# Small operations moved from VectorE to GpSimd and ScalarE in the middle of a decode block's forward and backward pass, and one buffer handed over an iteration later

## The chip, the cores and the metric

The kernel runs on one core of a Trainium2 chip. A core has five engines with an instruction queue each, worked off in order: TensorE (PE in the profile, with its weight loads as PEld), VectorE (DVE), ScalarE (ACT), GpSimd (POOL) and SyncE (SP). The engines wait for each other by semaphores. Transfers between the chip's memory (HBM) and the core's on-chip memory go through 16 DMA engines; they are issued from the queues of SP (loads), POOL (the two big gradients) and ACT (the smaller gradients). PE writes to PSUM, here eight banks; the other data lie in SBUF.

The metric is the device time of one execution in microseconds, as the median of several runs.

## The reference

The program computes a transformer block for two sequences at one new token each, and the gradients of its output. With B = 2, H = 32 heads, S = 4096 cached positions and a head size of 128:

```python
q = (layernorm(x) @ wq)                      # per head, 128 long
scores = einsum("bhqd,bhkd->bhqk", q, k) * Dh**-0.5
p = softmax(scores)
o = einsum("bhqk,bhkd->bhqd", p, v)
h = x + o @ wo
h2 = h + relu(layernorm(h) @ w1) @ w2
# outputs: h2, and the gradients for x, k_cache, v_cache, wq, wo, w1, w2
```

The caches are 2 x 32 x 4096 x 128 in bfloat16, 64 MB each. Both are read, and gradients of the same size are written: for a head, the gradient of V is the outer product of the probabilities `p` with the output's gradient `go`, and the gradient of K that of `p * (V go - p.(V go))` with q.

## The kernel before, in words

A head's K or V is one tile of 128 partitions x 32 blocks x 128 (1 MB). There are 64 pairs of batch and head.

**First pass.** `p1_iter(i, ...)` is a generator that interleaves three pairs: pair `i` (its K tile is transposed by PE in four groups, `pair_transpose`, copied from PSUM by ScalarE, and multiplied with q, `pair_matvec`, to give the scores `s` and the row maximum `rmax`), pair `i-1` (PE spreads the maximum, `mx`; VectorE reduces it to `nb`; ScalarE makes `ep` = exp; VectorE makes `pk` = K times e in two halves of 16 blocks, `pk_half(0)` and `pk_half(1)`; the copy of e into `pk`'s extra column, `pk_tile`, is done by GpSimd before iteration `P2_AT` and by ScalarE from there on; `P_bf` keeps e for later), and pair `i-2` (PE multiplies V with `pk`, eight calls of `m_part`, into the single bank `m`, and sums `u` in `u_part`; ScalarE copies the result out as `MT` and `OU`). The generator yields eight times an iteration, at positions k = 0 to 7. The K tile of pair `i-1` is given back after `pk_half(1)`, the V tile of pair `i-2` at the end.

**The middle.** After the 32 pairs of batch 0 a background generator, `middle_gen(0)`, computes the rest of the forward pass for this batch and the beginning of the backward pass: the output projection, the second layernorm, the MLP, and then groups of heads, `go_group`, which turn the gradient of the attention's output into `goc`, `gom` (through `pair_rows`: two small PE products and four copies out of PSUM), `negdot` and `GQc`. Its large VectorE instructions are the multiply-and-sum rows of `ttr`; how many of them go into an iteration is set by `slot`. `o_group` scales four heads' outputs.

**Second pass.** It begins at iteration `P2_AT` = 41, with one turn `j` in two iterations: `p2_iter` makes `rb` and `pp`, the products of V with `go`, and gV in two halves of VectorE; `p2_tail` makes `gsp` and gK in two halves. GpSimd issues the write of a gradient tile as soon as VectorE has made its second half. When the first pass has ended (iteration 65), the second goes on alone, with the weights' gradients beside it. The V tiles of the last six heads of batch 0 are kept from the first pass, so that the first turns load nothing.

**What sets the order.** The program is written out by hand in the order in which each engine shall work: `plan` pairs iterations `i` with turns `j`, and the tables `LIGHT`, `HEAVY` and `HEAVY_TAIL` say after which position k of an iteration a step of the second pass is put. Thirteen 1 MB buffers are shared by the tags "ld" (loads) and "g" (gradients); `give(tile, to)` hands a buffer to a tag, and `pump()` issues loads in a fixed order as far as "ld" has buffers, in the order in which they were given back. A load waits on SyncE until its buffer's last reader is done.

`p1_iter` and `pk_half` are at lines 483 and 495 of the kernel before, `pair_rows` at 348, `o_group` at 621, `go_group` at 701, and the main loop's choice of positions at 1278.

Of the kernel before, what the change touches and what calls it, by code (L numbers as in the profile page):

```python
# [7 lines left out]
FP32 = mybir.dt.float32  # L8
BF16 = mybir.dt.bfloat16
ALU = mybir.AluOpType  # L10
ACT = mybir.ActivationFunctionType
# [4 lines left out]
def kernel(  # L16
# [20 lines left out]
    nc = tc.nc  # L37

    B, Sq, D = A_x.shape
    _, H, Sk, Dh = A_k_cache.shape  # L40
# [4 lines left out]
    NSC = Sk // 128  # L45
# [3 lines left out]
    SCALE = 0.08837890625  # L49
# [3 lines left out]
    HALF = NSC // 2  # L53
    GH = 8
    OG = 4
# [12 lines left out]
    small = ctx.enter_context(tc.tile_pool(name="small", bufs=3))  # L68
# [5 lines left out]
    def pst(shape, dtype, role, name):  # L74

        k = banks[role].pop(0)
        banks[role].append(k)
        return ps.tile(shape, dtype, tag=f"bank{k}", bufs=1, name=name)
# [19 lines left out]
    def goes_to(tag):  # L98

        if owned[tag] > wanted.get(tag, len(pools)):  # L100
            for other in homes:
                if owned[other] < wanted.get(other, 0):
                    return other
        return tag

    def give(t, to=None, first=False):
        tag, k, _ = home_of.pop(id(t))
        to = to or goes_to(tag)
        owned[tag] -= 1
        owned[to] += 1  # L110
        free[to] += 1
        homes[to].insert(0 if first else len(homes[to]), k)
        given_at[k] = step[0]
# [86 lines left out]
    OFc = cols.tile([128, H, B], BF16)  # L200
    GQc = cols.tile([128, H, B], BF16)
    qsc = cols.tile([128, H, B], BF16)
    goc = cols.tile([128, H, B], BF16)

    gom = cols.tile([128, B, H, 2, 2], BF16)
    nc.gpsimd.memset(gom[:], 0.0)
    qm = gom
    negdot = cols.tile([128, H, B], FP32)
    OU = cols.tile([128, B, H], FP32)
    Uc = cols.tile([128, B, H], FP32)  # L210
    rt = cols.tile([128, B, H], FP32)
    asum = cols.tile([128, B, ND], FP32)
    nc.vector.memset(asum[:], 0.0)
    P_bf = cols.tile([128, NPS, NSC], BF16)
# [130 lines left out]
    w1_t = wts.tile([128, ND, Dff], BF16)  # L345
    wo_r = A_wo.rearrange("(c p) d -> p c d", p=128)

    def pair_rows(dst, src, hs, bs):

        n, nb = hs.stop - hs.start, bs.stop - bs.start  # L350
        t = pst([128, 2, n, nb], FP32, "mid", "pr_ps")
        for par in range(2):
            nc.tensor.matmul(t[:, par, :, :], lhsT=sel[:, par, :, :].rearrange("p c k -> p (c k)"),
                             rhs=src[:, hs, bs], start=True, stop=True)
        for c in range(2):
            rows = slice(64 * c, 64 * c + 64)
            for par in range(2):
                nc.vector.tensor_copy(out=dst[rows, bs, hs, par, c].rearrange("p b h -> p h b"), in_=t[rows, par, :, :])

    WO_PARTS = (0, H // 4, H // 2, 3 * H // 4, H - OG, H)  # L360

# [47 lines left out]
    NP1 = len(pairs)  # L409
# [6 lines left out]
    p_slot = {bh: n for n, bh in enumerate(pairs[:NPS])}  # L416
# [66 lines left out]
    def p1_iter(i, dve_group, busy):  # L483

        c = S1[i] if i < NP1 else None
        p = S1[i - 1] if 1 <= i <= NP1 else None
# [7 lines left out]

        def pk_half(k):

            sl = slice(k * HALF, (k + 1) * HALF)
            nc.vector.tensor_tensor(  # L498
                out=p["pk"][k][:, :, 0:128].rearrange("p s (a two) -> p s a two", two=2),
                in0=p["K"][:, sl, :].rearrange("p s (a two) -> p s a two", two=2),  # L500
                in1=p["ep"][:, sl, None, :].to_broadcast([128, HALF, 64, 2]), op=ALU.mult)

        def pk_tile(k):

            pk = pkp.tile([128, HALF, 130], BF16, tag="pK", bufs=3, name="pk")
            col, e = pk[:, :, 128:129], p["ep"][:, k * HALF:(k + 1) * HALF, 0:1]
            if i < P2_AT:
                nc.gpsimd.tensor_copy(out=col, in_=e)  # L508
            else:
                nc.scalar.copy(out=col, in_=e)  # L510
            p["pk"].append(pk)
# [12 lines left out]
        if c is not None:  # L524
            b, h = pairs[i]
# [4 lines left out]
        if r is not None:  # L530
            r["m"] = pst([128, 132], FP32, "m", "m_ps")
        m_first = r is not None and H + 1 < i < P2_AT + 3
        if m_first:
            m_part(0)
        if p is not None:

            bp, hp = pairs[i - 1]
# [9 lines left out]
        if p is not None:  # L547
            ep = pkp.tile([128, NSC, 2], BF16, tag="ep", bufs=3, name="ep")
            nc.scalar.activation(out=ep[:], in_=p["s"][:, :, None].to_broadcast([128, NSC, 2]),  # L549
                                 func=ACT.Exp, bias=nb[:], scale=SCALE, accum_out=es[:, bp, hp:hp + 1])  # L550
# [9 lines left out]
        if p is not None:  # L560
            pk_half(0)
# [18 lines left out]
        if p is not None:  # L580
            pk_tile(1)
            if hp % OG == OG - 1:
                nc.vector.reciprocal(out=rt[:, bp, hp + 1 - OG:hp + 1], in_=totp)
            (nc.gpsimd if i < P2_AT else nc.vector).tensor_copy(out=P_bf[:, p_slot[(bp, hp)], :], in_=ep[:, :, 0])
            pk_half(1)
            give(p["K"], "g" if i in (P2_AT, NP1) else None, i == NP1)
        if r is not None:
            m_part(5)
            m_part(6)
# [31 lines left out]
    def o_group():  # L621
        b, g = divmod(o_next[0], H // OG)
        hs = slice(g * OG, g * OG + OG)
        nc.vector.tensor_tensor(out=OU[:, b, hs], in0=OU[:, b, hs], in1=rt[:, b, hs], op=ALU.mult)
        nc.vector.tensor_copy(out=OFc[:, hs, b], in_=OU[:, b, hs])
        o_next[0] += 1

    def a_group():
# [10 lines left out]
    def a_heads(i):  # L639
# [3 lines left out]
        if o_next[0] < NP1 // OG and i >= o_next[0] * OG + OG + 2:  # L643
            b, g = divmod(o_next[0], H // OG)
            if i >= (O_AT[g] if b == 0 else P2_AT + 2):
                o_group()
# [37 lines left out]
    def ttr(in0, in1, acc, width, kc=128, junk=None):  # L684
        if junk is None:
            junk = rows3[:, 0, :]
        nc.vector.tensor_tensor_reduce(out=junk[0:kc, 0:width], in0=in0, in1=in1, scale=1.0, scalar=0.0,  # L687
                                       op0=ALU.mult, op1=ALU.add, accum_out=acc)
# [3 lines left out]
    def turn():  # L692

        while slot[0] <= 0:
            yield 0.0
        slot[0] -= 1
# [4 lines left out]
    def go_group(b, h0, h1, hbc):  # L701

        hs = slice(h0, h1)
        n = h1 - h0
        go32 = small.tile([128, GH], FP32, tag="go32", bufs=1, name="go32")
        for k in range(n):
            yield from turn()
            ttr(wo_t[:, h0 + k, :], hbc, go32[:, k:k + 1], D)
            yield 0.9
        nc.vector.tensor_copy(out=goc[:, hs, b], in_=go32[:, 0:n])  # L710
        pr = small.tile([128, GH], FP32, tag="pr", bufs=1, name="pr")
        nc.vector.tensor_tensor(out=pr[:, 0:n], in0=goc[:, hs, b], in1=OU[:, b, hs], op=ALU.mult)
        yield from wait(2 + b)
        pair_rows(gom, goc, hs, slice(b, b + 1))
        yield from wait(2)
        d_ps = pst([128, 2, GH], FP32, "mid", "d_ps")
        nc.tensor.matmul(d_ps[:, 0, 0:n], lhsT=ones_f32, rhs=pr[:, 0:n], start=True, stop=True)
        for k in range(n):
            h = h0 + k
            MT, side, slot_mt = MTs.pop((b, h))  # L720
            nc.tensor.matmul(d_ps[:, 1, k:k + 1], lhsT=MT[:], rhs=goc[:, h, b:b + 1], start=True, stop=True)
            mt_free[side].append(slot_mt)
        nc.vector.tensor_scalar(out=negdot[:, hs, b], in0=d_ps[:, 0, 0:n], scalar1=-1.0, scalar2=None, op0=ALU.mult)
        ud = small.tile([128, GH], FP32, tag="ud", bufs=1, name="ud")
        nc.vector.tensor_tensor(out=ud[:, 0:n], in0=Uc[:, b, hs], in1=negdot[:, hs, b], op=ALU.mult)
        mg = small.tile([128, GH], FP32, tag="mg", bufs=1, name="mg")
        nc.vector.tensor_tensor(out=mg[:, 0:n], in0=d_ps[:, 1, 0:n], in1=rt[:, b, hs], op=ALU.mult)
        nc.vector.tensor_tensor(out=ud[:, 0:n], in0=mg[:, 0:n], in1=ud[:, 0:n], op=ALU.add)
        nc.vector.tensor_scalar(out=GQc[:, hs, b], in0=ud[:, 0:n], scalar1=SCALE, scalar2=None, op0=ALU.mult)
        for h in range(h0, h1):  # L730
            done.add(("go", b, h))
        yield
# [154 lines left out]
    NSB = 8  # L887
# [251 lines left out]
    def bg_until(mark):  # L1139
        slot[0] = 99  # L1140
        forced[0] = True
        while mark not in done:
# [2 lines left out]

    M0_ITERS = 7
    P2_AT = H + 2 + M0_ITERS
    E0 = H - KEPT[0] + 3
    EARLY_T = {E0: [(0, 0)], E0 + 1: [(0, 1), (1, 0)], E0 + 2: [(0, 2)], E0 + 3: [(0, 3)],
               E0 + 4: [(1, 1)], E0 + 5: [(1, 2)], E0 + 6: [(1, 3)]}  # L1150
    RATES = (0.2, 0.8, 0.2, 0.8, 0.45)
# [4 lines left out]
    i = j = 0  # L1156
    while i <= NP1 + 1 or j <= NP1:
        ii = i if i <= NP1 + 1 else None
        jj = j if i >= NP1 or (i >= P2_AT and (i - P2_AT) % 2 == 0) else None
        plan.append((ii, jj))  # L1160
# [45 lines left out]
    HEAVY = {1: 1, 3: 1, 4: 1, 5: 1, 7: 1}  # L1206
    HEAVY_TAIL = {1: 1, 2: 1, 3: 1, 4: 1, 5: 1, 7: 1}
    LIGHT = {1: 1, 3: 1, 6: 1}
# [8 lines left out]
    for n, (i, j) in enumerate(plan):  # L1217
# [21 lines left out]
        open_tail = [k for k in S2 if "T3" in S2[k]]  # L1239
# [25 lines left out]
        if i is None:  # L1265
            spread[0] = 2
            at_k[0] = 1
            k = 0
# [6 lines left out]
                bg_step(1, RATE2[(0, 2, 0, 1)[sum(j >= a for a in RATE2_AT)]] * (0.4 if spreading[0] else 1.0))  # L1275
                bg_step(2, RATE3)
            continue
        at = LIGHT if j is None else HEAVY_TAIL if open_tail else HEAVY
        for k, _ in enumerate(p1_iter(i, i < H + 1, 0)):
            for _ in range(at.get(k, 0)):  # L1280
                if g2 is not None:
# [60 lines left out]
```

## Time and profile before

| | us |
|---|---|
| median of 3 runs | 893.32 |
| lowest and highest of them | 891.46, 894.52 |
| the profiled execution | 890.47 |
| its span, first to last instruction | 888.7 |

| engine | busy us | share of the span |
|---|---|---|
| PE | 731.7 | 82% |
| DVE | 687.7 | 77% |
| ACT | 469.3 | 53% |
| POOL | 203.9 | 23% |

The DMA engines moved 361.84 MB, 407 GB/s in the mean over the span; HBM was read for 211.11 MB and written for 149.13 MB. The granted clock of TensorE was 0.781 of full speed in the mean, 1.0 or nearly so up to some 440 us and 0.5 to 0.7 later.

Iteration i can be found in the trace by its instruction `nb`: iteration 37's starts at 233.58 us, that of 41 at 258.62, that of 45 at 287.60. An iteration of the first pass in the middle takes 5.9 to 6.7 us.

A line of a timeline gives the start and the duration in us, the engine, the kernel's line, the operation, output and inputs by their names in the program, the shapes, and in brackets how long the engine had been idle before and what ended this. An instruction's end can overlap the start of the next on the same engine. The profile of one execution is the source of all durations.

### The profile page before, as it was taken

How to read it: one execution, taken by the hardware profiler on the slowest of the kernel's cores; microseconds unless marked ns; L12 is line 12 of the kernel's file. 1: busy time of each engine (PE TensorE's matmuls, PEld its weight loads, DVE VectorE, ACT ScalarE, POOL GpSimd, SP SyncE). 2: the span in 40 equal slices, each digit the busy share in tenths (PEclk: the TensorE clock that was granted, in tenths of full speed). 3: DMA queues.
4: the chain of work that ended last, by engine and by line, in shares of the span. 5: the costliest groups of instructions: out<-in, count | busy, mean ns of one | idle time of the engine just before them, and what ended most of it. 6: DMA issues, size and time to landing. Idle time of an engine off the chain costs nothing. (4 is left out here: it accounts for less than half of the span.)

```text
span 888.7 us, 24642 instructions
## 1 busy us (share of the span) xinstructions
PE 731.7 (82%) x10145; PEld 614.4 (69%) x10145; DVE 687.7 (77%) x1283; ACT 469.3 (53%) x1184; POOL 203.9 (23%) x342
## 2 busy tenths in 40 slices
PE   4999899999998998988888668885888888658971
PEld 4887788889887887867777556664666675526560
DVE  2665779976899896886796888778988467899992
ACT  1443434445554565554446766553667765437761
POOL 1344334442310010000023322111322011111141
PEclk9999989999999999998985655656557755555575
DMA  9999999999999999999999999999999999999996
GB/s 377 418 412 404 408 407 420 411 414 408 356 369 362 421 423 423 424 422 423 423 383 419 419 419 416 416 415 420 398 409 414 420 423 424 423 427 421 423 422 256
DMA packets 56304, 361.84 MB, mean 407 GB/s; under 512 B 5696, under 2 KB 11904, under 8 KB 15488
## 3 DMA queue, kind: packets, MB, share of 16 engines
q1 hardware_dynamic: 34536, 211.13, 58.3%
q0 software_dynamic: 18432, 134.23, 36.4%
q10 hardware_dynamic: 3224, 14.92, 4.1%
q8 instruction: 80, 1.31, 0.6%
q14 instruction: 32, 0.26, 0.1%
HBM read 211.11 MB, written 149.13 MB: 405 GB/s over the span
## 5 line engine op out<-in xcount | busy, mean ns | idle before, releaser
L447 ACT COPY t_sb<-t_ps 128x512 f32<-128x512 f32 x471 | 267.3, 586 | 173.5 <-PE t_ps L442 168.1
L456 PEld LDWEIGHTS <-t_sb 128*128 128x128 bf16 x4032 | 165.9, 102 | 84.1 <-ACT t_sb L447 43.7
L442 PE MATMUL t_ps<-ident_f,Wt 128*128 128x128 f32 x832 | 196.4, 385 | 0.2 <-ACT t_sb L447 0.2
L498 DVE TENSOR_TENSOR pk<-Kt,ep 128x2048 bf16<-128x2048 bf16 x128 | 156.3, 1222 | 43.5 <-ACT ep L549 27.2
L491 PE MATMUL m_ps<-pk,Vt 128*128 128x129 bf16 x2048 | 175.8, 223 | 14.8 <-DMA Vt<-in_A_v_cache_dram 14.2
L861 DVE TENSOR_TENSOR gV<-rb,pp 128x2048 bf16<-128x2048 bf16 (+2 forms) x128 | 147.1, 1172 | 36.1 <-DMA out_dram<-gK 20.1
L861 DVE TENSOR_TENSOR gK<-rb,gsp 128x2048 bf16<-128x2048 bf16 x128 | 153.8, 1227 | 24.6 <-DMA out_dram<-gV 21.4
L442 PEld LDWEIGHTS t_ps<-ident_f,Wt 128*128 128x128 f32 x832 | 136.8, 200 | 31.5 <-issue 24.8
L442 PE MATMUL t_ps<-ident_f,Kt 128*128 128x128 f32 x1024 | 150.2, 281 | 5.3 <-DMA Kt<-in_A_k_cache_dram 5.0
L491 PEld LDWEIGHTS <-Vt 128*128 128x128 bf16 x2048 | 131.1, 99 | 18.2 <-DMA Vt<-in_A_v_cache_dram 16.2
L442 PEld LDWEIGHTS t_ps<-ident_f,Kt 128*128 128x128 f32 x1024 | 113.6, 145 | 6.9 <-issue 4.0
L508 POOL COPY pk<-ep 128x16 bf16<-128x16 bf16 x80 | 83.1, 1040 | 150.6 <-ACT ep L549 111.1
L456 PE MATMUL dp_ps<-gom,t_sb 128*128 128x2 bf16 x1984 | 92.9, 168 | 23.1 <-ACT t_sb L447 22.6
L942 POOL DMA_DIRECT2D out_dram<-gV x64 | 34.2, 534 | 310.0 <-DVE nb L541 111.9
L456 PE MATMUL s_ps<-gom,t_sb 128*128 128x2 bf16 x2048 | 79.8, 164 | 2.5 <-DVE t_sb L445 1.5
L882 POOL DMA_DIRECT2D out_dram<-gK x64 | 34.0, 531 | 198.6 <-DVE gK L861 153.5
L1009 ACT CAST ot<-o_ps 128x512 bf16<-128x512 f32 (+3 forms) x152 | 66.9, 496 | 8.0 <-DMA out_dram<-ot 6.9
L611 ACT CAST MT<-m_ps 128x128 bf16<-128x128 f32 x64 | 17.0, 266 | 101.7 <-PE m_ps L491 101.7
L903 ACT ACTIVATE rb<-dp_ps,rt 128x256 bf16<-128x256 f32 x64 | 30.1, 470 | 54.2 <-PE dp_ps L898 53.0
L687 DVE CUSTOM_DVE_ANT_0 rows<-wo_t,rows 128x640 bf16<-128x640 bf16 x64 | 52.3, 818 | 0.2
L687 DVE CUSTOM_DVE_ANT_0 rows<-wqs,gqr 128x1024 bf16<-128x1024 bf16 x40 | 48.8, 1219 | 0.2
L687 DVE CUSTOM_DVE_ANT_0 rows<-w_t,rows 128x640 bf16<-128x640 bf16 (+2 forms) x58 | 45.8, 790 | 0.7 <-DVE nb L541 0.2
(199 smaller groups left out, 729.1 us busy)
## 6 DMA issues: line engine op xcount, KB each, us to landing
Kt<-in_A_k_cache_dram SPq DMA_DIRECT2D x64, 1024.0 KB, 17.6
Vt<-in_A_v_cache_dram SPq DMA_DIRECT2D x64, 1024.0 KB, 16.7
out_dram<-gV POOLq DMA_DIRECT2D x64, 1024.0 KB, 15.1
out_dram<-gK POOLq DMA_DIRECT2D x64, 1024.0 KB, 15.7
Wt<-in_A_v_cache_dram SPq DMA_DIRECT2D x52, 1024.0 KB, 11.7
out_dram<-ot ACTq DMA_DIRECT2D x6, 960.0 KB, 12.7
wq_t<-in_A_wq_dram SPq DMA_DIRECT2D x5, 1024.0 KB, 11.0
wqs<-in_A_wq_dram SPq DMA_DIRECT2D x5, 1024.0 KB, 15.6
```

The lines of the kernel that those rows point to most:

```text
L442: nc.tensor.transpose(t_ps[:, j, :], natf[:, 2 * cc:2 * cc + 2, :].rearrange("p c k -> p (c k)"), ident_f[:])
L447: nc.scalar.copy(out=t_sb[:], in_=t_ps[:])
L456: nc.tensor.matmul(dst[:, sc:sc + 2], lhsT=v[:, j, :, par], rhs=vecs[:, par, :], start=(par == 0), stop=(par == 1))
L491: nc.tensor.matmul(r["m"][:, 0:129], lhsT=r["V"][:, sc, :], rhs=r["pk"][sc // HALF][:, sc % HALF, 0:129], start=(sc == 0), stop=(sc == NSC ...
L498: nc.vector.tensor_tensor(out=p["pk"][k][:, :, 0:128].rearrange("p s (a two) -> p s a two", two=2), in0=p["K"][:, sl, :].rearrange("p s (a ...
L508: nc.gpsimd.tensor_copy(out=col, in_=e)
L687: nc.vector.tensor_tensor_reduce(out=junk[0:kc, 0:width], in0=in0, in1=in1, scale=1.0, scalar=0.0, op0=ALU.mult, op1=ALU.add, accum_out=acc)
L861: nc.vector.tensor_tensor(out=pairs_view(dst[:, sl, :]), in0=row.rearrange("p (a two) -> p a two", two=2)[:, None, :, :].to_broadcast([128 ...
L882: nc.gpsimd.dma_start(out=natural(out_2, bp, hp), in_=gK[:])
L903: nc.scalar.activation(out=rb[:], in_=bank[:, 128:384], func=ACT.Copy, scale=rt[:, b, h:h + 1])
L942: nc.gpsimd.dma_start(out=natural(out_3, b, h), in_=gV[:])
L1009: nc.scalar.copy(out=ot[0:P, k, n0:n0 + nn], in_=o_ps[0:P, 0:nn])
```

## The change

Seven edits, all about iterations 37 to 46 and the groups of heads:

- `pk_half(1)` in iterations 37 to 44 makes 12 of its 16 blocks on VectorE. GpSimd copies the four remaining e into a float32 column each (`ef`), and ScalarE multiplies the four blocks of K by them.
- `P_bf` is copied by GpSimd up to iteration 46 instead of 40.
- `o_group` runs on GpSimd for batch 1, but for its last group.
- Of the four copies to `gom` in `pair_rows`, ScalarE makes two, for the groups of batch 0.
- In `go_group`, `ud` (twice) and `GQc` move to GpSimd.
- The K tile that is handed to the gradients is that of iteration 42 instead of 41.
- In iteration 42 the two halves of gK come behind `pk_half(1)` (both at position 5) instead of at positions 3 and 6.

```diff
-    def pair_rows(dst, src, hs, bs):
+    def pair_rows(dst, src, hs, bs, split=False):
...
-                nc.vector.tensor_copy(out=dst[rows, bs, hs, par, c].rearrange("p b h -> p h b"), in_=t[rows, par, :, :])
+                d = dst[rows, bs, hs, par, c].rearrange("p b h -> p h b")
+                if split and par == 1:
+                    nc.scalar.copy(out=d, in_=t[rows, par, :, :])
+                else:
+                    nc.vector.tensor_copy(out=d, in_=t[rows, par, :, :])
...
-            sl = slice(k * HALF, (k + 1) * HALF)
+            n = HALF - (PKS if k == 1 and i in PKS_AT else 0)
+            sl = slice(k * HALF, k * HALF + n)
...
+            if n < HALF:
+                ef = small.tile([128, NSB], FP32, tag="pf", bufs=2, name="ef")
+                nc.gpsimd.tensor_copy(out=ef[:, 0:PKS], in_=p["ep"][:, NSC - PKS:NSC, 0])
+                for x in range(PKS):
+                    nc.scalar.activation(out=p["pk"][k][:, n + x, 0:128], in_=p["K"][:, k * HALF + n + x, :],
+                                         func=ACT.Copy, scale=ef[:, x:x + 1])
...
-            (nc.gpsimd if i < P2_AT else nc.vector).tensor_copy(out=P_bf[:, p_slot[(bp, hp)], :], in_=ep[:, :, 0])
+            (nc.gpsimd if i < P2_AT + 6 else nc.vector).tensor_copy(out=P_bf[:, p_slot[(bp, hp)], :], in_=ep[:, :, 0])
             pk_half(1)
-            give(p["K"], "g" if i in (P2_AT, NP1) else None, i == NP1)
+            give(p["K"], "g" if i in (P2_AT + 1, NP1) else None, i == NP1)
...
-        nc.vector.tensor_tensor(out=OU[:, b, hs], in0=OU[:, b, hs], in1=rt[:, b, hs], op=ALU.mult)
-        nc.vector.tensor_copy(out=OFc[:, hs, b], in_=OU[:, b, hs])
+        eng = nc.gpsimd if b == 1 and g < H // OG - 1 else nc.vector
+        eng.tensor_tensor(out=OU[:, b, hs], in0=OU[:, b, hs], in1=rt[:, b, hs], op=ALU.mult)
+        eng.tensor_copy(out=OFc[:, hs, b], in_=OU[:, b, hs])
...
-        pair_rows(gom, goc, hs, slice(b, b + 1))
+        pair_rows(gom, goc, hs, slice(b, b + 1), b == 0)
...
-        nc.vector.tensor_tensor(out=ud[:, 0:n], in0=Uc[:, b, hs], in1=negdot[:, hs, b], op=ALU.mult)
+        nc.gpsimd.tensor_tensor(out=ud[:, 0:n], in0=Uc[:, b, hs], in1=negdot[:, hs, b], op=ALU.mult)
...
-        nc.vector.tensor_tensor(out=ud[:, 0:n], in0=mg[:, 0:n], in1=ud[:, 0:n], op=ALU.add)
-        nc.vector.tensor_scalar(out=GQc[:, hs, b], in0=ud[:, 0:n], scalar1=SCALE, scalar2=None, op0=ALU.mult)
+        nc.gpsimd.tensor_tensor(out=ud[:, 0:n], in0=mg[:, 0:n], in1=ud[:, 0:n], op=ALU.add)
+        nc.gpsimd.tensor_scalar(out=GQc[:, hs, b], in0=ud[:, 0:n], scalar1=SCALE, scalar2=None, op0=ALU.mult)
...
+    PKS = 4
+    PKS_AT = range(H + 5, P2_AT + 4)
...
-        at = LIGHT if j is None else HEAVY_TAIL if open_tail else HEAVY
+        at = {1: 1, 5: 2, 7: 1} if i == P2_AT + 1 else LIGHT if j is None else HEAVY_TAIL if open_tail else HEAVY
```

## The prediction

> **What bounds the kernel now.** I read the page's slices first, then the windows by stage, then the engines' own timelines inside one stage. The slices, from the page (engine busy in tenths of 22.2 us, and what the DMA engines moved):
>
> ```profile
> DVE  2665779976899896886796888778988467899992
> ...
> DMA  9999999999999999999999999999999999999996
> GB/s 377 418 412 404 408 407 420 411 414 408 356 369 362 421 423 423 424 422 423 423 383 419 419 419 416 416 415 420 398 409 414 420 423 424 423 427 421 423 422 256
> ```
>
> Most of the span moves 408 to 425 GB/s: the kernel is bound by DMA. The hollow is slices 10 to 12 (222 to 289 us), 356 to 369 GB/s. Windows cut by stage (length, then busy us of PE, PEld, DVE, ACT, POOL, then clock, DMA share, GB/s):
>
> ```profile
> 232.00:240.00 8.00, 7.57 (x122) 6.67 (x120) 7.81 (x17) 4.98 (x15) 2.08 (x4) 1.00 0.87 339
> 240.00:246.00 6.00, 5.19 (x90) 4.44 (x89) 5.93 (x15) 2.97 (x8) 1.57 (x3) 1.00 0.90 325
> ...
> 263.00:269.00 6.00, 5.71 (x97) 4.99 (x95) 6.00 (x13) 3.52 (x11) 0.69 (x1) 1.00 0.97 384
> 269.00:272.00 3.00, 1.46 (x24) 1.20 (x22) 2.99 (x5) 1.17 (x3) 0.44 (x1) 1.00 0.45 117
> 272.00:277.00 5.00, 4.75 (x105) 4.20 (x105) 4.65 (x12) 2.17 (x8) 0.34 (x2) 1.00 0.98 341
> 277.00:287.00 10.00, 7.79 (x133) 6.76 (x132) 9.27 (x26) 4.47 (x13) 0.53 (x1) 1.00 1.01 425
> ```
>
> DVE is busy 13.74 of 14 us from 232 to 246, and 8.99 of 9 from 263 to 272, while the DMA has room. From 277 on the DMA is full again (425), so what is gained or lost before 277 is carried to the end, if the later stages stay full. The ceiling: at 425 GB/s the 14 us from 263 to 277 could carry 5.95 MB; the rows carry 384x6 + 117x3 + 341x5 = 4.36 MB. 1.59 MB, or 3.7 us, go unused there. From 232 to 246 it is (86x8 + 100x6)/425 = 3.0 us more.
>
> Why the DMA is empty at 269 shows in SyncE's issues, and the order of the chain around iteration 37 in the other engines' timelines (start, duration, engine, line):
>
> ```profile
> 262.59 0.33 SPq L478 DMA_DIRECT2D Kt<-in_A_k_cache_dram  x1
> 270.05 0.33 SPq L478 DMA_DIRECT2D Vt<-in_A_v_cache_dram  x1
> 270.46 0.55 SPq L478 DMA_DIRECT2D Kt<-in_A_k_cache_dram  x1
> 275.84 0.33 SPq L478 DMA_DIRECT2D Vt<-in_A_v_cache_dram  x1
> ```
>
> ```profile
> 236.62 0.80 POOL L584 COPY P_bf<-ep 128x32 bf16<-128x32 bf16 x1
> ...
> 238.03 0.27 ACT L611 CAST MT<-m_ps 128x128 bf16<-128x128 f32 x1 [0.48 <-PE m_ps L491]
> ...
> 238.14 1.22 DVE L498 TENSOR_TENSOR pk<-Kt,ep 128x2048 bf16<-128x2048 bf16 x1
> 239.28 0.19 DVE L597 TENSOR_REDUCE rmax<-s_ps 128x1 bf16<-128x32 f32 x1
> 239.38 0.82 DVE L687 CUSTOM_DVE_ANT_0 rows<-w_t,rows 128x640 bf16<-128x640 bf16 x1
> ...
> 238.70 0.40 PE L491 MATMUL m_ps<-pk,Vt 128*128 128x129 bf16 x4
> 239.53 0.23 PE L539 MATMUL s_ps<-neg_ident,rmax 128*128 128x128 bf16 x1 [0.43 <-DVE rmax L597]
> ```
>
> No load is issued for 7.5 us, because iteration 41's K tile goes to the gradients. And DVE sets the pace: PE waits for `rmax`.
>
> **Part 1: what leaves DVE, iterations 37 to 44.** Successive DVE starts give the prices.
> - K times e: 16 blocks take 1.14 us from start to start (238.14 to 239.28), so 4 of them 0.285; 8 iterations: 2.28 us.
> - `P_bf` in 41 to 44: 0.09 each (268.71 to 268.80): 0.36.
> - Half the `gom` copies of two head groups (0.48 for four in 272.51): 2 x 0.24 = 0.48.
> - `ud` twice and `GQc`, two groups: `negdot` at 257.16 to the next big one at 257.88 is 0.72 us for five; without three about 0.35 less each: 0.70.
> - `OU` and `OFc` of two groups: 0.39 (276.87 to 277.26) and 0.26: 0.65.
>
> Sum 4.47 us of DVE: 2.48 before iteration 43 (6 x 0.285, 2 x 0.09 and the first group's 0.59), 1.99 in 43 and 44. The same edits after 277 (P_bf of 45 and 46, later groups) lie under a full DMA: nothing, and if that cover were gone they would save some 0.1 to 0.7 each.
>
> **Part 2: what ScalarE and GpSimd take.** Four ScalarE blocks of 128x128: the gradient's like blocks take 0.386 us alone, 1.67 for six in a row, so 0.26 apart and about 1.15 for four. From 41 on they fit: between the copies at 260.84 and MT at 262.60 ScalarE idles 1.50 us, and `ef` comes early, since there ScalarE makes the pk column and GpSimd has only P_bf ahead of it. In 37 to 40 they don't: GpSimd first makes two pk columns and P_bf. `ef` has no row. Its near end is P_bf's shortest, 0.20 us; its far end P_bf's longest, 1.28. P_bf ended at 237.42, just as DVE's next big instruction began (237.39 to 238.21), and the GpSimd copies at 231.40 and 236.62 ended within 0.1 us of such a DVE instruction's end; I take one DVE instruction, `ef` at 238.25. So ScalarE's blocks run 238.3 to 239.4, and what queues behind them is MT (238.03 becomes 239.33), OU, both t_sb copies and the next `ep`; PE waits for MT and OU (one m bank) with its first m_ps group, which stands ahead of `mx`: 238.70 becomes 239.75, `mx` 240.0 instead of 239.53. DVE has a rows instruction to do until 239.84, so `nb` comes at 240.25 instead of 240.12: iteration 37 ends 0.13 later, not 0.28 earlier. By the same steps 38 adds 0.36 (its rows instructions are 0.62 and cover less), 39 nothing, 40 gives 0.4 back: it is relieved of 0.285 and the group's 0.59. PE, which stands 1.0 behind, costs 41 about 0.6 (pk waits for u_ps). So DVE stands 0.6 late at 266, where the removals alone would have it 1.7 to 2.1 early: the ScalarE wait eats part 1 there. In 43, 1.1 of the 1.36 removed (0.375, 0.59, 0.39) comes through, and it is 0.4 early at 280. Bounds of `ef`: at 0.20 nothing is late and some 1.9 us more are kept; at two DVE instructions about 1.0 us is lost in each of four iterations.
>
> ScalarE's two `gom` copies of a group, each like OU's 0.17, go into its idle time, 0.49 to 1.86 us ahead of MT: nothing; without that cover 0.34 twice.
>
> The other new GpSimd operations (`ud`, add, `GQc`, `OU`, `OFc`) lie in its queue ahead of the gV write: 3 to 5 of them at 0.20 to 1.28 us. That write may be issued up to 0.6 later; the DMA is full by then (425): 0, and at most 0.6 if it isn't. GpSimd copies that began just ahead of a DVE pk product (214.91 and 214.92) let it take 1.26 instead of 1.22: 22 such operations, at most 0.9 us, 0.2 taken and inside the rounding of the 0.4.
>
> By the Trainium skill (SBUF — State Buffer, SBUF: two separate sides) the pair of ports that both engines use is an exclusive lock, and whichever starts first keeps the other out for its whole instruction. The trace agrees where DVE is first (0.20 becomes 1.28); where GpSimd is first it doesn't (0.04 us lost, not 0.20). By that rule 22 operations would cost DVE up to 4.4 us, by the rows 0.9.
>
> **Part 3: the tile.** Iteration 41's K tile stays with the loads, 42's goes. gV of the first turn takes the tile of its own W, read until 261.64 by PE, and starts at 262.18: no wait. gK's two halves move behind pk's second half in 42 and wait for the ScalarE blocks that read the tile: up to 0.5 us of DVE (in the 0.6 to 0.7 late of 42 and 43), `rmax` 1.9 later, under PE's 0.92 us wait and DVE's rows instruction. SyncE gets one 1.05 MB load at some 263.5 instead of 270: 1.05/425 = 2.5 us of DMA time in an empty stretch. Bounds: 0, if the loads of 43 come as late as this one comes early (K's tile is free only after ScalarE's blocks, 275.84 becomes 276.8); 3.7, the whole hollow. I take 2.5, since 269 to 272 at 117 GB/s is empty enough for most of it.
>
> **The sum.** 2.5 + 0.4 = 2.9 us less. The profiled execution took 890.47 us (888.7 span and 1.8 around it) and would take 887.6; it lies 2.85 below the median shown, 893.32, which becomes 890.4.
>
> **Rivals.**
> - *More is kept.* If `ef` slips between two DVE instructions (0.20), iteration 43 starts some 1.2 early instead of 0.7 late, and the hollow from 232 shrinks: 2.9 + 1.9 = 4.8 less, 888.5. Against it: GpSimd's pk columns mean 1040 ns.
> - *The gap moves.* The early load lands early, the three of iteration 43 come 0.7 to 1.0 later, and the DMA is empty at 276 instead of 269; only 0.4 to 1.4 are left: 892.5. For it: the issues hang on ScalarE now.
> - *Slower: ScalarE's queue stalls in 37 to 40.* `ef` waits for a second DVE instruction (0.86 apart), MT starts 2.2 late, `mx` and `nb` 1.0 to 1.35: 4 x 1.35 = 5.4, less the 1.1 of 43 and gK's wait of 0.52 for its tile in 44 (282.85): 3.7 more, 897.0; the early load gains nothing, since nothing is in arrears when compute is this late. It decides from MT starting 1.6 us behind the last m_ps group on. For it: ScalarE's order is fixed and `ef` is last of four in GpSimd's.
> - *GpSimd holds DVE* by a full 0.20 on each of 22 operations: 890.4 + 4.4 = 894.8. The skill's lock would do this; the rows speak against it.
>
> **How the numbers follow.** The forecast 0.40, more kept 0.15, gap moved 0.23, stall 0.17, held 0.05. From no change a measurement of this kernel tells about 0.3%, 2.7 us (its three runs spread 3.1). The forecast's own range is 889 to 892, about two thirds below 890.6. Faster 0.15 + 0.27 + 0.03 = 0.45; same 0.13 + 0.18 + 0.02 = 0.33; slower 0.22, of stall, held and the tail of gap moved. The range from 888 to 895.5 leaves out half of the stall and a tail of more kept.
>
> **What would show it.** In the changed profile: a load issued near 263.5 and 269 to 272 above 300 GB/s; DVE's pk halves of 12 blocks near 0.93 us; `ef` ending within 0.9 us of P_bf; MT in 37 to 39 starting 1 to 1.6 us behind its m_ps; 277 onward at 420 or more, and every later stage 2 to 3 us earlier. The forecast is wrong if MT lags more, if 276 to 279 shows the hollow instead, or if a later stage (the one at 444 to 466 us, 383 GB/s, or the tail at 256) takes the gain back.

## The result, and the profile after

The changed kernel takes 899.88 us (median of 6 runs, 898.35 to 902.93); the kernel before took 891.46 (890.12 to 894.52) beside it. The ratio is 1.0093, 95% interval 1.0067 to 1.0119: slower by 0.93%, where the prediction had 890.4 us (2.9 below the median in its table) and a range from 888 to 895.5. The profiled execution took 901.73 us, with a span of 900.0 (before: 890.47 and 888.7).

The page's slices of the changed kernel (22.5 us each):

```profile
GB/s 378 418 411 406 409 408 419 410 415 410 334 354 228 409 424 423 422 424 423 423 389 425 421 417 418 419 419 404 396 418 396 423 425 425 424 427 423 424 415 230
```

Slice 12, counted from 0 (270 to 292 us), moves 228 GB/s, where the kernel before had 362. From slice 13 on the row is close to that of before: the loss is made in one place and carried to the end, as the prediction said it would be for a gain. The windows of the changed kernel in that place (length, then busy us of PE, PEld, DVE, ACT, POOL, then clock, DMA share, GB/s):

```profile
263.00:269.00 6.00, 6.00 (x121) 5.39 (x118) 5.99 (x11) 4.36 (x15) 1.57 (x2) 1.00 1.01 386
269.00:272.00 3.00, 1.89 (x31) 1.72 (x29) 1.27 (x2) 1.78 (x8) 1.31 (x2) 1.00 1.00 284
272.00:277.00 5.00, 0.27 (x4) 0.09 (x2) 0.00 (x0) 0.80 (x2) 0.00 (x0) 0.85 0.97 406
277.00:281.00 4.00, 0.67 (x7) 0.68 (x8) 3.19 (x5) 0.00 (x0) 0.53 (x1) 0.50 0.03 14
281.00:285.00 4.00, 4.00 (x57) 3.78 (x54) 2.19 (x7) 2.33 (x8) 0.95 (x6) 0.50 0.64 262
285.00:289.00 4.00, 4.00 (x74) 3.20 (x73) 3.19 (x8) 2.29 (x9) 0.76 (x1) 0.91 0.23 39
```

The hollow of 269 to 272 has been filled (284 GB/s instead of 117). Then, from 272 to 277, the DMA engines are full and the compute engines stand nearly still: VectorE does nothing in 5 us, PE 0.27 us of work and ScalarE 0.80. After that the DMA is empty twice. The timeline of the changed kernel says what VectorE waited for (start, duration, engine, line; in brackets the idle time before and what ended it):

```profile
267.43 0.78 POOL L954 DMA_DIRECT2D out_dram<-gV  x1 [5.05 <-DVE nb L552]
...
277.81 2.36 DVE L873 TENSOR_TENSOR gK<-rb,gsp 128x2048 bf16<-128x2048 bf16 x2 [7.54 <-DMA out_dram<-gV]
...
280.33 0.29 PE L550 MATMUL s_ps<-neg_ident,rmax 128*128 128x128 bf16 x1 [8.06 <-DVE rmax L608]
280.47 0.54 POOL L894 DMA_DIRECT2D out_dram<-gK  x1 [10.17 <-DVE rmax L608]
```

The first gK is held for 7.54 us by the *write of the first gV*. That write was issued at 267.43 and came to its end only as gK began. `rmax` stands behind gK in VectorE's new order, PE waits for `rmax` (8.06 us), and the K and V tiles stay occupied, so SyncE has no buffer to load into (it waits 16.5 us for a `pk` of VectorE):

```profile
264.37 0.33 SPq L482 DMA_DIRECT2D Kt<-in_A_k_cache_dram  x1
264.79 0.38 SPq L482 DMA_DIRECT2D Vt<-in_A_v_cache_dram  x1
269.91 0.33 SPq L482 DMA_DIRECT2D Kt<-in_A_k_cache_dram  x1
287.19 0.33 SPq L482 DMA_DIRECT2D Vt<-in_A_v_cache_dram  x1
```

The early load that the change is about does come (264.79, where the kernel before issued its next load at 270.05), but after the one at 269.91 none is issued for 17.3 us. Iteration 42, from its `nb` to the next, lasts 14.38 us instead of 7.01.

**Why gK waits for gV's write** stands in the kernel's own list of buffers, which the tags keep in order of return:

```python
k = homes[tag].pop(0)                                       # take: from the front
...
homes[to].insert(0 if first else len(homes[to]), k)         # give: to the end
```

In the kernel before the gradients' list held K's tile of iteration 40 (its number in program order; the one handed over at iteration 41), then the buffer of the turn's own W, when the first gV was taken: gV got the first, gK the second. The timeline of the kernel before fits: gK starts 1.88 us after gV's write was issued and waits for nothing.

```profile
262.18 1.23 DVE L861 TENSOR_TENSOR gV<-rb,pp 128x2048 bf16<-128x2048 bf16 x1
...
265.70 0.69 POOL L942 DMA_DIRECT2D out_dram<-gV  x1 [9.93 <-DVE nb L541]
...
267.58 1.22 DVE L861 TENSOR_TENSOR gK<-rb,gsp 128x2048 bf16<-128x2048 bf16 x1
```

In the changed kernel K's tile is not yet there when the first gV is taken. gV gets W's buffer, and gives it back, by program order, in iteration 41 as soon as its write is issued. K's tile is given in iteration 42, behind it in the list. So the first gK, taken right after, pops gV's buffer, whose write has just been issued, while the free K tile stands second. The name "buffer free" means two things: the program may take it, and its last reader, here a 1 MB write, is done.

That the write took 10 us fits the loads that it shared the DMA with: the loads of 264.37, 264.79 and 269.91 are 3.1 MB beside its 1.05, and at the 386, 284 and 406 GB/s of the windows the stretch from 267.43 to 277 carries 0.61 + 0.85 + 2.03 = 3.5 MB. The early load itself is part of what the write had to share with. (Of the 64 writes of gV in the kernel before, the median lands 15.1 us after its issue.)

### The profile page after: what moved, and what is told of

Read it like the earlier page. It is cut to its first block, busy times and chain, and to the rows that moved or that the text cites. A ratio compares the mean times of both kernels' runs of the same rounds, so it can differ in the third digit from the quotient of the medians.

```text
span 900.0 us, 24707 instructions
## 1 busy us (share of the span) xinstructions
PE 737.7 (82%) x10145; PEld 619.1 (69%) x10145; DVE 677.8 (75%) x1218; ACT 478.8 (53%) x1228; POOL 239.1 (27%) x403
## 5 line engine op out<-in xcount | busy, mean ns | idle before, releaser
L503 DVE TENSOR_TENSOR pk<-Kt,ep 128x2048 bf16<-128x2048 bf16 (+1 forms) x128 | 154.2, 1206 | 48.6 <-ACT ep L560 30.0
L873 DVE TENSOR_TENSOR gV<-rb,pp 128x2048 bf16<-128x2048 bf16 (+2 forms) x128 | 147.2, 1172 | 32.1 <-DMA out_dram<-gK 16.5
L446 PE MATMUL t_ps<-ident_f,Kt 128*128 128x128 f32 x1024 | 153.6, 286 | 3.0 <-DMA Kt<-in_A_k_cache_dram 2.5
L446 PEld LDWEIGHTS t_ps<-ident_f,Kt 128*128 128x128 f32 x1024 | 116.1, 148 | 4.7 <-PE m_ps L495 1.7
```

Source lines behind the costliest of these rows:

```text
L446: nc.tensor.transpose(t_ps[:, j, :], natf[:, 2 * cc:2 * cc + 2, :].rearrange("p c k -> p (c k)"), ident_f[:])
L503: nc.vector.tensor_tensor(out=p["pk"][k][:, 0:n, 0:128].rearrange("p s (a two) -> p s a two", two=2), in0=p["K"][:, sl, :].rearrange("p s ...
L873: nc.vector.tensor_tensor(out=pairs_view(dst[:, sl, :]), in0=row.rearrange("p (a two) -> p a two", two=2)[:, None, :, :].to_broadcast([128 ...
```

## The experiments

At the outset there were two theories. Theory L, the landing: gK waits for the write of gV, and this is nearly all of the loss; it hangs on the tile edits alone. Theory Q, the queues: the operations moved to ScalarE and GpSimd cost the time, and the wait for the write only shows what was late already. Later expectations divide Q into theory S (ScalarE's order: the four blocks stand in front of MT) and theory G (GpSimd's order), and then ask for `ef` and for `gom` by name. Ratios are to the kernel before, measured beside each version.

**The tile edits alone** (the rest as before):

```diff
-            give(p["K"], "g" if i in (P2_AT, NP1) else None, i == NP1)
+            give(p["K"], "g" if i in (P2_AT + 1, NP1) else None, i == NP1)
...
-        at = LIGHT if j is None else HEAVY_TAIL if open_tail else HEAVY
+        at = {1: 1, 5: 2, 7: 1} if i == P2_AT + 1 else LIGHT if j is None else HEAVY_TAIL if open_tail else HEAVY
```

> The kernel before with the two edits of the tile alone: iteration 42's K tile goes to the gradients instead of 41's, and gK's halves stand behind pk's second half there; no operation changes its engine. Theory L (landing): buffers are taken from the front of the gradients' list and given back to its end, so the first gK gets the buffer of the first gV and waits until that write has landed, about 7.5 us of DVE; it expects 7 to 9 us more than before and a DVE wait of 7 us or more at iteration 42. Theory Q (queues): the moved operations on ScalarE and GpSimd cost the time; it expects this kernel within 2.5 us of before.

Measured: 898.63 us, ratio 1.0079 (1.0064 to 1.0094), 7.0 us more, as theory L expects. Its timeline shows the same wait with no edit of ScalarE or GpSimd present:

```profile
265.42 0.69 POOL L954 DMA_DIRECT2D out_dram<-gV  x1 [9.73 <-DVE nb L552]
...
275.89 2.36 DVE L873 TENSOR_TENSOR gK<-rb,gsp 128x2048 bf16<-128x2048 bf16 x2 [7.30 <-DMA out_dram<-gV]
```

**All but the tile edits** (the change with these two lines as before):

```diff
-            give(p["K"], "g" if i in (P2_AT + 1, NP1) else None, i == NP1)
+            give(p["K"], "g" if i in (P2_AT, NP1) else None, i == NP1)
...
-        at = {1: 1, 5: 2, 7: 1} if i == P2_AT + 1 else LIGHT if j is None else HEAVY_TAIL if open_tail else HEAVY
+        at = LIGHT if j is None else HEAVY_TAIL if open_tail else HEAVY
```

> The changed kernel with the tile's two edits undone (iteration 41's K tile goes to the gradients, gK's halves at positions 3 and 6); all moved operations stay on GpSimd and ScalarE. Theory L expects no wait of gK at iteration 42 and a time from 2 us less to 1 us more than before. Theory Q expects 5 to 9 us more than before, as the whole change has.

Measured: 892.63 us, ratio 1.0013 (1.0003 to 1.0023), some 1.2 us more: far from theory Q's 5 to 9 and just beyond the 1 us that theory L allowed. The two halves add up: 0.79% and 0.13% are 0.92%, against 0.93% for the whole.

**The tile edits alone, with K's tile put at the front of the list**, so that gK takes it and no write is waited for:

```diff
-            give(p["K"], "g" if i in (P2_AT + 1, NP1) else None, i == NP1)
+            give(p["K"], "g" if i in (P2_AT + 1, NP1) else None, i in (P2_AT + 1, NP1))
```

> As the kernel with the tile's edits alone, but iteration 42's K tile is put at the front of the gradients' list, so that the first gK takes it and not the buffer of the first gV. Theory L expects the wait to be gone: 0 to 3 us less than before, since one load of 1.05 MB (2.5 us at 425 GB/s) is issued 5 us earlier. If the time stays 5 us or more above before, the later place of gK in the order costs it and not the landing.

Measured: 891.01 us, ratio 0.9990 (0.9979 to 1.0001). One argument takes back 7.6 us. In the timeline gK starts with no wait, and SyncE's issues show what the tile edits do once the buffer is right:

```profile
268.22 2.36 DVE L873 TENSOR_TENSOR gK<-rb,gsp 128x2048 bf16<-128x2048 bf16 x2
...
261.61 0.33 SPq L482 DMA_DIRECT2D Kt<-in_A_k_cache_dram  x1
262.10 0.33 SPq L482 DMA_DIRECT2D Vt<-in_A_v_cache_dram  x1
267.48 0.33 SPq L482 DMA_DIRECT2D Kt<-in_A_k_cache_dram  x1
275.39 0.33 SPq L482 DMA_DIRECT2D Vt<-in_A_v_cache_dram  x1
275.81 0.83 SPq L482 DMA_DIRECT2D Kt<-in_A_k_cache_dram  x1
276.73 0.90 SPq L482 DMA_DIRECT2D Vt<-in_A_v_cache_dram  x1
```

Two loads come earlier (262.10 and 267.48 instead of 270.05 and 270.46), and then none for 7.9 us. By 277 there are six, as many as in the kernel before (262.59 to 276.89). The pause in the loads has moved by one iteration.

**The whole change with the tile at the front** (the same one argument):

> The whole change, with iteration 42's K tile put at the front of the gradients' list. The instructions and their order are those of the change; only gK's buffer differs. Theory L expects 1 to 4 us less than before (my sum of 2.9 was made for this assignment of buffers) and DVE idle for less than 1 us at iteration 42. Theory Q expects 5 us or more above before still.

Measured: 893.66 us, ratio 1.0029 (1.0014 to 1.0044). This is neither theory L's 1 to 4 us less nor theory Q's 5 or more above. 5.7 us of the loss of 8.3 are back; a smaller loss of 2.6 us stays, which the tile edits do not make (they give 0.9990 alone). The next runs look for it.

**Which of the moved operations.** Each of the next two adds one group to the tile edits with the tile at the front: the split of the pk product, and the GpSimd moves (`P_bf`, `OU`, `OFc`, `ud`, `GQc`).

```diff
-    PKS_AT = ()
+    PKS_AT = range(H + 5, P2_AT + 4)
```

> The kernel with the tile's edits and the tile at the front of the list (891.0 us, level with before), and of the moved operations only the four blocks of K times e on ScalarE in iterations 37 to 44. Theory S (ScalarE's order): the four blocks stand ahead of MT, so PE waits for the m bank, and what DVE saves is lost again; it expects 1 to 3 us more than that kernel, iteration 42 some 1 us late. Theory G (GpSimd's order): the small operations ahead of the gradients' writes cost; it expects 0 to 2 us less here.

Measured: 890.86 us, ratio 0.9988 (0.9978 to 0.9998). Theory S, as far as the split alone goes, falls: it had 1 to 3 us more than the version without the split (0.9990).

```diff
-            (nc.gpsimd if i < P2_AT else nc.vector).tensor_copy(out=P_bf[:, p_slot[(bp, hp)], :], in_=ep[:, :, 0])
+            (nc.gpsimd if i < P2_AT + 6 else nc.vector).tensor_copy(out=P_bf[:, p_slot[(bp, hp)], :], in_=ep[:, :, 0])
...
-        eng = nc.vector
+        eng = nc.gpsimd if b == 1 and g < H // OG - 1 else nc.vector
...
-        nc.vector.tensor_tensor(out=ud[:, 0:n], in0=Uc[:, b, hs], in1=negdot[:, hs, b], op=ALU.mult)
+        nc.gpsimd.tensor_tensor(out=ud[:, 0:n], in0=Uc[:, b, hs], in1=negdot[:, hs, b], op=ALU.mult)
...
```

> The same base, and of the moved operations only those on GpSimd (P_bf up to iteration 46, OU and OFc of batch 1, ud, the sum and GQc); K times e whole on DVE, all gom copies on DVE. Theory S expects 0 to 2 us less than the base, since 2.2 us of DVE work leave iterations 40 to 44. Theory G expects 1 to 3 us more: a gradient's write is issued later behind them.

Measured: 890.63 us, ratio 0.9991 (0.9979 to 1.0002). Theory G, with 1 to 3 us more, falls too. Neither group costs anything alone.

**The whole change with the tile at the front, without the split** (GpSimd moves and the split of `gom`):

```diff
-    PKS_AT = range(H + 5, P2_AT + 4)
+    PKS_AT = ()
```

> The whole change with the tile at the front, but K times e whole on DVE; so GpSimd's operations and the two gom copies on ScalarE. In the change's trace the gom copies of DVE and ScalarE ran one behind the other (0.2 us of waiting twice). If that costs, this is 0.5 to 1.5 us slower than the kernel with GpSimd's operations alone; else within 0.5 us of it. Theory S expects 1 to 3 us less than with the split.

Measured: 892.01 us, ratio 0.9999 (0.9984 to 1.0013). So the split of the pk product costs 0.3% when the GpSimd moves and the split of `gom` are there, and nothing when neither is. (`gom`'s split without it is 0.08% above the GpSimd moves alone, inside the intervals.) The traces show one reason, in iteration 42. First the whole change with the tile at the front:

```profile
266.69 2.10 DVE L503 TENSOR_TENSOR pk<-Kt,ep 128x2048 bf16<-128x2048 bf16 x2
266.73 1.24 POOL L595 COPY P_bf<-ep 128x32 bf16<-128x32 bf16 x1
267.93 0.90 POOL L509 CAST ef<-ep 128x4 f32<-128x4 bf16 x1
...
268.86 1.28 ACT L511 ACTIVATE pk<-Kt,ef 128x128 bf16<-128x128 bf16 x4 [1.21 <-POOL ef L509]
270.17 2.36 DVE L873 TENSOR_TENSOR gK<-rb,gsp 128x2048 bf16<-128x2048 bf16 x2 [1.38 <-ACT pk L511]
```

Then the version with the split alone, where `P_bf` is VectorE's from iteration 41 on:

```profile
265.98 1.29 POOL L509 CAST ef<-ep 128x4 f32<-128x4 bf16 x1
266.02 1.22 DVE L503 TENSOR_TENSOR pk<-Kt,ep 128x2048 bf16<-128x2048 bf16 x1
...
267.30 1.28 ACT L511 ACTIVATE pk<-Kt,ef 128x128 bf16<-128x128 bf16 x4 [0.32 <-POOL ef L509]
268.61 2.36 DVE L873 TENSOR_TENSOR gK<-rb,gsp 128x2048 bf16<-128x2048 bf16 x2 [0.42 <-ACT pk L511]
```

With both, `ef` stands behind `P_bf` on GpSimd. `P_bf` is held through VectorE's first product (1.24 us instead of 0.2), `ef` through the second (0.90), and it ends at 268.83, when VectorE's two products have ended. gK is written into the very K tile that ScalarE still reads, so VectorE waits 1.38 us, with `rmax` behind it. With the split alone the wait is 0.42. Iteration 42 lasts 8.23 us in the first version, 7.32 in the second and 7.14 without the split: the late `ef` costs 0.9 to 1.1 us there. The issue of gV's write (0.78 us) stands ahead of `P_bf` in GpSimd's queue, and `P_bf` begins just after the first product has.

The Trainium skill (SBUF — State Buffer, SBUF: two separate sides) says that whichever of VectorE and GpSimd starts first on their shared ports keeps the other out for its whole instruction. In this direction, with VectorE first, the trace agrees: two small copies end as VectorE's two products do.

**`ef` ahead of everything else on GpSimd, and all `gom` copies on VectorE** (from the whole change with the tile at the front):

```diff
+            if k == 0 and i in PKS_AT:
+                p["ef"] = small.tile([128, NSB], FP32, tag="pf", bufs=2, name="ef")
+                nc.gpsimd.tensor_copy(out=p["ef"][:, 0:PKS], in_=p["ep"][:, NSC - PKS:NSC, 0])
             if i < P2_AT:
                 nc.gpsimd.tensor_copy(out=col, in_=e)
...
-                ef = small.tile([128, NSB], FP32, tag="pf", bufs=2, name="ef")
-                nc.gpsimd.tensor_copy(out=ef[:, 0:PKS], in_=p["ep"][:, NSC - PKS:NSC, 0])
+                ef = p["ef"]
...
-                if split and par == 1:
+                if False:
```

> The whole change with the tile at the front, but GpSimd copies ef ahead of both pk columns and of P_bf, and all gom copies are on DVE. If the wait for ef is what costs in ScalarE's queue, MT starts within 0.6 us of its m_ps in iterations 38 to 40 and the time is 1 to 3 us below the whole change with the tile at the front (893.7). If the 1.2 us of the four blocks themselves cost, it is within 0.5 us of that.

Measured: 889.71 us, ratio 0.9978 (0.9968 to 0.9988): faster than both kernels, and more of a gain on the whole change with the tile at the front than the 1 to 3 us expected. In iteration 42 `ef` is now first, and the order of the waits changes:

```profile
265.90 1.22 POOL L519 CAST ef<-ep 128x4 f32<-128x4 bf16 x1
...
267.08 0.95 POOL L597 COPY P_bf<-ep 128x32 bf16<-128x32 bf16 x1
...
267.16 1.28 ACT L510 ACTIVATE pk<-Kt,ef 128x128 bf16<-128x128 bf16 x4 [0.33 <-POOL ef L519]
...
268.47 2.36 DVE L875 TENSOR_TENSOR gK<-rb,gsp 128x2048 bf16<-128x2048 bf16 x2 [0.51 <-ACT pk L510]
```

**Which of its two edits.** From the whole change with the tile at the front, only the copies of `gom` back on VectorE:

```diff
-                if split and par == 1:
+                if False:
```

> The whole change with K's tile put at the front of the list, but with all twelve blocks of gom copied by VectorE, as in the kernel before; ef still comes late, behind P_bf on GpSimd. Theory ef (the late ef is what made the whole change 1.5 to 3 us worse than the version with ef ahead): no gain from this alone, 892.5 to 893.7 us. Theory gom (the copies of gom that ran one behind the other on two engines are it): the gain is here already, 889.5 to 890.7 us. In between (891 to 892.3) both take part.

Measured: 891.71 us, ratio 1.0003 (0.9992 to 1.0013): in the range where both take part. And the reverse, `ef` ahead with the copies of `gom` split again:

```diff
-                if False:
+                if split and par == 1:
```

> The fastest version so far (ef ahead of the pk columns and of P_bf on GpSimd, tile at the front), with the blocks of gom split between VectorE and ScalarE again. Theory ef: as fast as without the split, 889.3 to 890.3 us. Theory gom: 1 to 3 us slower, 891 to 893 us.

Measured: 889.96 us, ratio 0.9991 (0.9979 to 1.0004), inside theory ef's range. By the ratios, `ef` ahead brings 0.38% with the copies split and 0.25% without; the copies on VectorE bring 0.26% with `ef` late and 0.13% with `ef` ahead. `ef` is the larger part. For the smaller one the intervals lie apart with `ef` late and overlap with `ef` ahead, so by the times alone it isn't settled.

The traces say more. The first group's copies fall into iteration 40. First the whole change with the tile at the front, then the same with the copies on VectorE:

```profile
255.59 0.16 ACT L360 CAST gom<-pr_ps 64x2 bf16<-64x2 f32 x1 [1.12 <-DVE gom L362]
...
256.17 1.28 ACT L511 ACTIVATE pk<-Kt,ef 128x128 bf16<-128x128 bf16 x4
```

```profile
257.02 1.28 ACT L511 ACTIVATE pk<-Kt,ef 128x128 bf16<-128x128 bf16 x4 [1.04 <-POOL ef L509]
```

VectorE's first copy starts at 255.41 in the one and at 256.92 in the other. So the four blocks start 0.76 us behind it where ScalarE's two copies stand ahead of them, and 0.10 us behind it where they do not; MT and the rest of ScalarE's queue follow the blocks. The split copies run one behind the other on the two engines (255.41, 255.59, 255.78, 255.98), so they relieve VectorE of little. The lengths of the two iterations, each from one trace:

| version, tile at the front | iteration 40, us | iteration 42, us |
|---|---|---|
| whole change | 6.72 | 8.23 |
| copies of `gom` on VectorE | 6.17 | 8.22 |
| `ef` ahead, copies split | 6.40 | 7.34 |
| `ef` ahead, copies on VectorE | 5.84 | 7.35 |

The split of `gom` costs 0.55 us in iteration 40, with `ef` late or ahead. Without the four blocks behind it, it costs 0.07 there (6.18 with the split, 6.11 with the GpSimd moves alone). The late `ef` costs 0.32 us in iteration 40 and 0.88 in 42.

**The fastest version with the tile edits undone:**

```diff
-            give(p["K"], "g" if i in (P2_AT + 1, NP1) else None, i in (P2_AT + 1, NP1))
+            give(p["K"], "g" if i in (P2_AT, NP1) else None, i == NP1)
...
-        at = {1: 1, 5: 2, 7: 1} if i == P2_AT + 1 else LIGHT if j is None else HEAVY_TAIL if open_tail else HEAVY
+        at = LIGHT if j is None else HEAVY_TAIL if open_tail else HEAVY
```

> The fastest version so far with the tile edits undone: K's tile goes to the gradients at iteration 41, as in the kernel before, and W's loads stand at the positions of before. If the later giving with the tile at the front is worth its earlier 1.05 MB load (the prediction's 2.5 us): 891.5 to 892.5 us. If it is worth nothing, as the tile edits alone with the tile at the front (0.9990 of the kernel before) suggest: 889.3 to 890.5 us.

Measured: 891.09 us, ratio 0.9998 (0.9984 to 1.0013). Beside the fastest version's 0.9978 this says that the tile edits with the right buffer are worth 0.2%, some 1.8 us; beside the whole change (1.0029 with them, 1.0013 without) they cost 0.16%; alone they give 0.1%. The three do not agree in sign, and in each pair the intervals overlap. So no worth of the tile edits is shown, only that it lies within some 2 us of nothing.

**The fastest version once more**, since the best of several is partly the luckiest:

> The fastest version so far (ef ahead of the pk columns and of P_bf, all gom copies on VectorE, tile at the front), measured a second time. If its gain is real: 0.9970 to 0.9990 of the kernel before, 888.7 to 890.6 us. If it was the luckiest of several versions that are all equal to the kernel before: 0.9990 to 1.0010.

Measured: 889.87 us, ratio 0.9984 (0.9970 to 0.9999). The gain of 0.16 to 0.22%, 1.4 to 2.0 us, is there twice, and both intervals leave out 1. It is smaller than what the prediction called measurable from its three runs.

## Why the prediction was wrong, point by point

**The bound.** Right. The kernel is bound by DMA outside the hollow, and what is lost before 289 us is carried to the end: `nb` of iteration 43 stands 9.1 us later than in the kernel before and that of iteration 50 still 9.2. (1.5 us of it are there at iteration 37's start, ahead of the first edit; in the other versions this point varies between -0.5 and +1.5.)

**Part 1, what leaves VectorE.** Right in its prices: twelve blocks take 0.95 us, 0.87 from start to start, where 0.855 was worked out. `gom` was not: split copies take as long as before, because they take turns, and ScalarE's share, which the prediction put at nothing, costs 0.55 us in iteration 40, where the four blocks queue behind it.

**Part 2, ScalarE in 37 to 40.** Right in its mechanism, too dark in its size. In the changed kernel's iteration 37:

```profile
238.08 0.81 POOL L595 COPY P_bf<-ep 128x32 bf16<-128x32 bf16 x1
238.83 0.18 POOL L509 CAST ef<-ep 128x4 f32<-128x4 bf16 x1
```

and on ScalarE, in the same iteration:

```profile
239.05 1.28 ACT L511 ACTIVATE pk<-Kt,ef 128x128 bf16<-128x128 bf16 x4
240.23 0.25 ACT L622 CAST MT<-m_ps 128x128 bf16<-128x128 f32 x1
```

`ef` slipped between two VectorE instructions (0.18 us, the near end of the bounds) instead of taking a whole one. MT follows the four blocks, as said. Iterations 37 and 38 became 0.25 and 0.08 shorter, where 0.13 and 0.36 longer was forecast. From there it goes the other way: 39 and 40 became 0.10 and 0.01 longer (nothing, and 0.4 shorter, was forecast), 41 0.48 longer (about 0.6). So the changed kernel stands 0.26 later at iteration 42 than at 37, where 0.6 to 0.7 was forecast at 266 us. The kernel without the tile edits, which shows this part by itself, stands 0.8 later at 42 and 0.7 earlier at 44 (0.4 forecast at 280); that it comes near the forecast is luck, since iteration 41 alone adds 1.0 there.

**Part 2, ScalarE from 41 on.** Wrong: "`ef` comes early, since there ScalarE makes the pk column and GpSimd has only P_bf ahead of it". In 42 GpSimd also has the issue of gV's write (0.78 us) ahead of it, and `P_bf` and `ef` are each held through a VectorE product. The wait of gK for ScalarE's blocks was forecast as up to 0.5 us; it measured 1.38 in the whole change with the tile at the front (in the changed kernel gV's write hides it), and 0.42 to 0.51 where `ef` was not behind `P_bf`.

**Part 3, the tile.** Here is the step that failed. "Iteration 41's K tile stays with the loads, 42's goes" is right; the step after it, that gK's halves "wait for the ScalarE blocks that read the tile", takes gK's buffer to be K's tile. The prediction asked only who still reads this tile, and priced the rest at 2.5 us gained. It looked at gV's wait (none, and there is none) and not at which buffer gK pops from the list. It pops gV's. The wait was worth 7.54 us in the profiled execution, and putting the tile at the front takes 0.89% off the tile edits (1.0079 to 0.9990) and 0.64% off the whole change. The sum was therefore wrong by a term it did not contain, of three times the size of the one that it took in this place.

The 2.5 us themselves were also too large. With the right buffer the tile edits alone bring 0.9 us (from 1.9 less to 0.1 more), inside "only 0.4 to 1.4 are left" of the rival *the gap moves*; the issue times show that mechanism, six loads by 277 either way. Its reason was partly another: not the issues that hang on ScalarE, which does no more than before in that version, but that the loads are one buffer short an iteration later.

**The rivals.** *More is kept* and *the gap moves* are each true of one part, with the landing taken away. *The stall* does not happen with the size given: the split alone is at 0.9988. *GpSimd holds VectorE* does not either: in the version with the GpSimd moves alone, which has all of the 22 but the eight `ef`, VectorE's pk products from 220 to 295 us take 1.219 us in the mean, and 1.220 in the version without the moves. (The ratio, 0.9991, says less, since 2.2 us of VectorE's work leave as well.) The lock works in the other direction: GpSimd is held, and through `ef` it holds ScalarE and then VectorE. No rival was about a new wait for a transfer out of a buffer (*the stall* counts the 0.52 us that gK waits in iteration 44 of the kernel before), although the page of the kernel before lists such waits for later stages, gK and gV behind each other's writes.

**What stays open.** Of the 2.6 us that the whole change with the tile at the front is slower than the kernel before, the traces show about 0.9 for the late `ef` in iteration 42, and in iteration 40 0.3 for `ef` and 0.55 for the copies of `gom`. How much of these reaches the end, and where the rest comes from, is not shown.

## What to carry to other kernels

When an edit changes when a buffer is handed over, write down the list of free buffers at every take, in program order, and for each the last reader with the time at which it will be done; a buffer whose write has only been issued is not free, and under a full DMA a 1 MB write took 10 us here beside three loads of the same size. A take from the front of a first-in-first-out list gets the oldest return, not the readiest one, and one argument (`first`) was worth 5.7 to 7.9 us. A tiny operation on a slow queue, such as `ef`, belongs ahead of the larger ones when a second engine and then a third wait for it; a small operation added to a queue that works in order, such as ScalarE's copies of `gom`, delays what stands behind it by its own wait too.

## What the runs showed of the hardware

The pause made the next iteration slower too. The windows of the changed kernel from the middle of the pause on:

```profile
273.00:275.00 2.00, 0.00 (x0) 0.00 (x0) 0.00 (x0) 0.00 (x0) 0.00 (x0) 1.00 1.02 422
275.00:277.00 2.00, 0.00 (x0) 0.00 (x0) 0.00 (x0) 0.00 (x0) 0.00 (x0) 0.62 0.89 377
...
284.00:285.00 1.00, 1.00 (x19) 0.91 (x16) 0.02 (x1) 0.50 (x1) 0.00 (x0) 0.50 0.01 0
285.00:286.00 1.00, 1.00 (x12) 0.21 (x11) 0.23 (x1) 0.23 (x2) 0.00 (x0) 0.64 0.00 0
286.00:287.00 1.00, 1.00 (x32) 1.00 (x33) 1.00 (x2) 1.00 (x5) 0.00 (x0) 1.00 0.00 0
```

TensorE's last product before the pause ended at about 272.3. Its granted clock falls to 0.50 at about 275.5, 3.2 us later, and is full again only at 285.7, 5.4 us after the work resumed at 280.33. PE is busy without a break from 282 to 287, until 285.7 at half its clock:

```profile
284.15 1.03 PE L495 MATMUL m_ps<-pk,Vt 128*128 128x129 bf16 x8
...
286.55 0.63 PE L495 MATMUL m_ps<-pk,Vt 128*128 128x129 bf16 x8
```

VectorE waits 1.75 us for `u`, and iteration 43 is 0.95 us longer than before (8.62 us; 7.81 with the tile at the front, where there is no such pause): this pause cost somewhat more than its own length. In the run with the tile edits alone the clock falls 2.3 us after the last product and is full 3.1 us after the work resumes. By the Trainium skill (TensorE: Matmul & The Clock Gate, Part 1: The HAM clock gate) the clock is halved after at least one idle window of about 3.4 us and restored after at least one busy one, the windows running freely. The traces agree with the two states and roughly with the times, but not closely: both falls come earlier than a whole such window after the last product, and one return takes 5.4 us, the other 3.1.

GpSimd's time for the same small copy depends on what VectorE does at that moment: `ef` took 0.18 us in iteration 37 and 0.90 to 1.29 in 42, and `P_bf` 0.21 to 1.24.
